# A normalised FNet + gated-MLP block: the first tile's load, its roundings and the order of the first products

## The chip, the cores and the metric

One core of a Trainium2 chip runs the kernel. The core has five engines with instruction queues of their own: TensorE (PE; its weight loads are shown as PEld), VectorE (DVE), ScalarE (ACT), GpSimd (POOL) and SyncE (SP). DMA transfers are issued from the queues of SyncE, ScalarE and GpSimd. The metric is the device time of one execution in microseconds (us). Rows of the profile count from the start of the profiled span.

## The reference, cut to what matters

```python
xn = (x - mean(x)) / sqrt(var(x) + 1e-5)            # x: 2048 x 640, over the last axis
a  = xn @ dft_hid_re.T ;  b = xn @ dft_hid_im.T     # 640 x 640
y  = dft_seq_re @ a - dft_seq_im @ b                # 2048 x 2048
gate = xn @ W_gate ;  up = xn @ W_up                # 640 x 1728
out = x + y + ((gate * (gate > 0)) * up) @ W_down   # 1728 x 640
```

All arrays are float32.

## The kernel before, in words

The products with the sequence DFT matrix come first: for each group of 256 tokens (two tiles j = 0, 1 of 128 tokens each) the normalised x is the stationary operand, 128 x 128, and a piece of 512 columns of the DFT matrix (a chunk, c) is the moving one. To keep float32 accuracy each operand is split into a high part, rounded to TensorE's 32-bit format, and a low part, what the rounding left out; a product is made of three: high x times high DFT, low x times high DFT, high x times low DFT. In the code these are v = 0, 1 and 2.

The work is listed as steps (load, prepare, run, finish), which `drive` emits in a fixed order; instructions passed through `pin` keep the order in which they are written on their engine.

The head is the part before TensorE has work. TensorE runs 44 small products (L119) to warm up. `first_stream.load` issues the first DMAs: tile 0 of x in two halves by columns, one from SyncE's queue and one from ScalarE's (L613), then tile 0's piece of chunk 0 on SyncE's queue and of chunk 1 on ScalarE's (`lead_dft`, L610), then tile 1 and its pieces on SyncE's queue. Ahead of them VectorE sets the last column of tile 0's place to zero (L611); the DMA that covers that column waits for it. `first_group` then prepares:

- VectorE: statistics of each half (`ln_stats`, L211) and their aggregate (L212);
- ScalarE: one over the root of the variance (`ln_first`, L217);
- the high part of chunk 0, tile 0: columns 0 to 255 on ScalarE, 256 to 511 on VectorE (L346, L347; ScalarE's shows under `copy`, L128);
- `raw_high(0)`, VectorE (L337): high part of the normalised x, 384 columns;
- `center(0)`, ScalarE: minus the mean (`ln_mean`, L220) and x minus mean over all 640 columns (L342);
- `high(1, 0)`, ScalarE (L332): high part of chunk 1; `low(0, 0, ...)`, VectorE (L333): low part of chunk 0;
- `ln_refine`, VectorE (L226): three one-column steps of scalar_tensor_tensor that make the root more accurate; `ln_low`, VectorE (L240): low part of the normalised x, which needs `center` and `ln_refine`;
- `low(1, 0, ...)`, GpSimd (L333): low part of chunk 1. It is put behind a VectorE memset of one element of its own output (L354), so that it starts when VectorE has come that far.

Then the same for tile 1. `first_products(j, b)` (L576) issues tile j's products in a written order of (v, chunks); each entry has three products (x blocks 0, 1 and 4) into three banks. The entries are 18 products for tile 0 and 18 for tile 1. `next_products` (L546) follows with the next group.

GpSimd also makes low parts of later groups (L281), beside which VectorE runs `ln_center` (L230) on 640 columns in some groups.

Of the kernel before, what the change touches and what calls it, by code (L numbers as in the profile page):

```python
# [7 lines left out]
F32 = mybir.dt.float32  # L8
# [4 lines left out]
P = 128  # L13
S, D, F = 2048, 640, 1728
# [49 lines left out]
def fnet_reglu_kernel(  # L64
# [56 lines left out]
    def bank():  # L121
        return psum_p.tile([P, CH], F32, name="ps")
# [4 lines left out]
    def copy(o, i):  # L127
        return nc.scalar.activation(o, i, AF.Copy)  # L128
# [64 lines left out]
    def ln_place(g):  # L193
# [2 lines left out]
        b = g % NH * SG * D  # L196
        return late["ln_tile"][:, b : b + SG * D].rearrange("p (j d) -> p j d", j=SG)

    def ln_tiles(g):
        return (ln_place(g),  # L200
                small.tile([P, SG, 2, nc.vector.BN_STATS_DIM], F32, name="bs"),
                small.tile([P, SG, 7], F32, name="mv"))

    def ln_load(g, js):
# [2 lines left out]

    def ln_stats(g, xs, bs, mv, js):
        for j in range(SG)[js]:
            for i in range(2):  # L210
                yield nc.vector.bn_stats(bs[:, j, i], xs[:, j, i * D // 2 : (i + 1) * D // 2])  # L211
            yield nc.vector.bn_aggr(mv[:, j, 0:2], bs[:, j])  # L212

    def ln_first(g, mv, js):

# [6 lines left out]
    def ln_refine(g, mv, js):  # L222

        v, r0, t = (mv[:, js, i] for i in (1, 4, 5))
        for o, i, by, op in ((t, v, EPS, OP.add), (t, t, -0.5, OP.mult), (stat[:, 1, g, js], t, 1.5, OP.add)):
            yield nc.vector.scalar_tensor_tensor(o, i, by, r0, op0=op, op1=OP.mult)  # L226
# [20 lines left out]
    def pin(steps):  # L247
        return [tc.keep_in_program_order(i) for i in steps]
# [78 lines left out]
    def first_group(b):  # L327


        xs, bs, mv = ln_tiles(0)  # L330
        part = lambda c, j: b[c][1][:, j * CH : (j + 1) * CH]
        high = lambda c, j: pin([nc.scalar.activation(b[c][0][:, 0, j], part(c, j), AF.Copy)])  # L332
        low = lambda c, j, engine: pin([engine.tensor_tensor(b[c][0][:, 1, j], part(c, j), b[c][0][:, 0, j].bitcast(F32),  # L333
                                                             op=OP.subtract)])
        j0, j1 = slice(0, 1), slice(1, 2)
        def raw_high(j):
            pin([nc.vector.tensor_scalar(ln_parts(0, j, K14)[0], xs[:, j, K14], mv[:, j, 0:1], mv[:, j, 4:5],  # L337
                                         op0=OP.subtract, op1=OP.mult)])

        def center(j):  # L340
            pin([ln_mean(0, mv, slice(j, j + 1))])
            pin([nc.scalar.activation(xs[:, j], xs[:, j], AF.Identity, bias=stat[:, 0, 0, j : j + 1])])  # L342

        pin(ln_stats(0, xs, bs, mv, j0))
        pin([ln_first(0, mv, j0)])
        for cs, rounded in ((slice(0, HC), copy), (slice(HC, CH), nc.vector.tensor_copy)):  # L346
            pin([rounded(b[0][0][:, 0, 0, cs], part(0, 0)[:, cs])])  # L347
        raw_high(0)
        center(0)
        high(1, 0)  # L350
        low(0, 0, nc.vector)
        pin(ln_refine(0, mv, j0))
        pin([ln_low(0, xs, 0, K14)])
        pin([nc.vector.memset(b[1][0][:, 1, 0, :1].bitcast(F32), 0.0)])  # L354
        low(1, 0, nc.gpsimd)
        pin(ln_stats(0, xs, bs, mv, j1))
        high(0, 1)
        pin([ln_first(0, mv, j1)])
        raw_high(1)
        high(1, 1)  # L360
        center(1)
        pin(ln_refine(0, mv, j1))
        low(0, 1, nc.vector)
        pin([ln_low(0, xs, 1, K14)])
        pin([nc.vector.memset(b[1][0][:, 1, 1, :1].bitcast(F32), 0.0)])
        low(1, 1, nc.gpsimd)
# [200 lines left out]
    def first_products(j, b):  # L567

        keys = [("e1", 0), ("e1", 1), "v1"]
        for v, cs in (((0, (0,)), (2, (0,)), (0, (1,)), (1, (0, 1)), (2, (1,))),  # L570
                      ((0, (0, 1)), (1, (0, 1)), (2, (0, 1))))[j]:
            for c in cs:
                for d, key in zip((0, 1, 4), keys):
                    if j == 0 and v == 0:
                        E[c, key] = bank()
                    pin([nc.tensor.matmul(E[c, key], xn_part(j, d)[v == 1], b[c][0][:, int(v == 2), j],  # L576
                                          start=j == 0 and v == 0, stop=False)])

    def resident(g, d):
        return lambda j, i: xn_part(g * SG + j, d + i)  # L580
# [18 lines left out]
    def first_stream(c, name, g):  # L599

        t = {}
        half = int(name == "B21")
        n = half * NH + g

        norm = {0: 0 if n == 0 else None, 1: n + 1 if n < NG - 1 else None}.get(c)

        def load():
            if n == 0 and c == 0:
                st = start["raw"] = [raw(), raw()]
                get = lambda c, j, queue=nc.sync: pin([queue.dma_start(st[c][:, j * CH : (j + 1) * CH], lead_dft[c, j, :, :CH])])  # L610
                pin([nc.vector.memset(ln_place(0)[:, 0, D - 1 :], 0.0)])  # L611
                for queue, cs in ((nc.sync, slice(0, D // 2)), (nc.scalar, slice(D // 2, D))):
                    pin([queue.dma_start(ln_place(0)[:, 0, cs], x[: SG * P].rearrange("(p j) d -> p j d", j=SG)[:, 0, cs])])  # L613
                get(0, 0)
                get(1, 0, nc.scalar)
                pin([nc.scalar.activation(root_t, eps_t, AF.Abs_reciprocal_sqrt)])
                ln_load(0, slice(1, 2))
                get(0, 1)
                get(1, 1)
                return  # L620
            if norm is not None:
                tc.keep_in_program_order(ln_load(norm, slice(0, SG)))
            if n > 0 or c > 1:
                t["s"] = raw()
                nc.sync.dma_start(t["s"], dft[c, 0, n])
                start[c, n] = t

        def prepare():
            if norm == 0:
                start["b"] = [(parts(), st) for st in start["raw"]]  # L630
                first_group(start["b"])
                return
            if (n > 0 or c > 1) and "b" not in t:
                t["b"] = b = parts()
                with ExitStack() as order:
                    if c == 1:
                        order.enter_context(tc.issue_after(late["ln"]))
                        order.enter_context(tc.issue_after(late["high"]))
                    i = split(flat(b, 0), flat(b, 1), t["s"])
                if c == 1 and n < NG - 1:  # L640
                    late["ln"] = i.ins
                    scale_a21()
            if norm is not None:
                t1 = start[0, norm]
                t1["b"] = parts()
                next_group(norm, t1["b"], t1["s"], flat(b, 1)[:, W2 - 1 : W2] if norm > 1 else None)

        def run():
            if n == 0 and c < 2:
                first_products(c, start["b"])  # L650
                return
            if n > 0 and c == 0:
                next_products(n, t["b"])
                if n == NH - 1:
                    keep_first()
                return
            accs = [(c, ("e1", i)) for i in range(2)]
            with ExitStack() as order:
                if n > 0 and c == 1:
                    order.enter_context(tc.issue_after(start["pe"]))  # L660
                product(g, t["b"], resident(n, 0), accs, half == 0, half == 1, ((c, "v1"), half, half == 0))

        def keep_first():
            t["first"] = sums_a()
            for i, key in enumerate((("e1", 0), ("e1", 1), "v1")):
                pin([copy(t["first"][:, i], E[c, key])])
            late["finish"]()

        def finish():
            if g == NH - 1:  # L670
                s = t.get("first")
                if s is None:
                    s = (sums_a, sums_b)[c % 2]()
                    for i, key in enumerate((("e1", 0), ("e1", 1), "v1")):
                        copy(s[:, i], E[c, key])
                defer(1, lambda: nc.gpsimd.dma_start(pqd[c][0][:, :3] if half else firsts[c], s[:, :3]))

        todo.append((load, prepare, run, finish))
# [225 lines left out]
    class Weights:  # L904
# [36 lines left out]
        def low(self, src, at, n, o):  # L941
            main = lambda t: t.rearrange("p (k n) -> p k n", k=n)[:, :, : 2 * P]
            tt(self.w[:, o : o + n * 2 * P].rearrange("p (k n) -> p k n", k=n), main(src), main(self.w[:, at : at + n * P3]).bitcast(F32),  # L943
               op=OP.subtract)
# [574 lines left out]
```

## Time and profile before

| | |
|---|---|
| median of 3 runs | 1019.25 us (1019.0 to 1019.42) |
| profiled execution | 1019.12 us |
| its span (first to last instruction) | 1017.3 us |
| TensorE busy | 1012.6 us |
| VectorE, ScalarE, GpSimd busy | 809.2, 488.4, 135.3 us |
| granted TensorE clock, mean | 1.00 |

The span is the profiled execution's time less what lies around the instructions. Busy times of different engines overlap. A row of a timeline has start, duration, engine, line, operation, output and input by the program's names, shapes, and in brackets the engine's idle time ahead of it with what ended that.

### The profile page before, as it was taken

The page shows a single profiled execution, that of the slowest core. Times are in us where ns is not written, and L with a number is a line of the kernel's source. Part 1 is how long each engine was busy: PE and PEld are TensorE (multiplying, and loading weights), DVE is VectorE, ACT ScalarE, POOL GpSimd, SP SyncE. Part 2 cuts the span into 40 slices and gives each one's busy share as a digit, 9 for nine tenths or more (in the row PEclk, how much of TensorE's full clock was granted, in tenths as well). Part 3 has the DMA queues.
Part 4 walks back from the last instruction along what each step waited for, and adds up shares of the span by engine and source line. Part 5 has one row for each costly group of instructions (what it writes and reads, how often), then busy time and mean ns, then how long its engine had stood idle before and what let it go on. Part 6 is the DMA issues. An engine that isn't in the chain of part 4 may idle for free.

```text
span 1017.3 us, 12622 instructions
## 1 busy us (share of the span) xinstructions
PE 1012.6 (100%) x4498; PEld 838.8 (82%) x4498; DVE 809.2 (80%) x1085; ACT 488.4 (48%) x659; POOL 135.3 (13%) x215
## 2 busy tenths in 40 slices
PE   9999999999999999999999999999999999999998
PEld 8888888888888888888888888888888888888887
DVE  7957977998989677787777988886687896767983
ACT  5654453343443334555556655565444434444432
POOL 3521001012121001222221011001000000000000
PEclk9999999999999999999999999999999999999999
DMA  8997735968979898666569877784898467896724
GB/s 321 319 293 278 267 120 172 336 217 273 349 237 353 338 358 269 232 236 220 205 214 390 291 273 284 278 308 151 318 387 288 132 243 245 285 331 203 244 79 138
DMA packets 94142, 266.43 MB, mean 262 GB/s; under 512 B 11776, under 2 KB 32832, under 8 KB 91264
## 3 DMA queue, kind: packets, MB, share of 16 engines
q1 hardware_dynamic: 73584, 185.12, 52.8%
q0 software_dynamic: 20064, 79.97, 21.5%
q8 instruction: 35, 0.57, 0.2%
q10 hardware_dynamic: 432, 0.56, 0.2%
q14 instruction: 27, 0.22, 0.1%
HBM read 198.74 MB, written 65.81 MB: 260 GB/s over the span
## 4 chain that ended last, share of the span: by engine, by line
PE 99%; DMA 0%; DVE 0%; SPq 0%; ACT 0%; issue 0%
PE ps L137 29%; PE ps L139 29%; PE ps L138 29%; PE ps L973 4%; PE ps L546 3%; PE ps L976 2%; PE ps L576 1%; PE ps L1364 1%; PE ps L1369 0%; DMA raw<-in_lead 0%; PE ps L1379 0%; DVE xs_early L337 0%; SPq L613 0%; ACT y L128 0%; DVE cb L347 0%
## 5 line engine op out<-in xcount | busy, mean ns | idle before, releaser
L131 ACT ACTIVATE cb<-rw 128x1024 fp32r<-128x1024 f32 x83 | 81.8, 988 | 138.0 <-PE ps L139 92.5
L132 DVE TENSOR_TENSOR cb<-rw,cb 128x1024 fp32r<-128x1024 f32 x83 | 93.8, 1131 | 48.2 <-ACT cb L131 47.7
L131 ACT ACTIVATE cb<-raw 128x1024 fp32r<-128x1024 f32 x71 | 75.3, 1060 | 114.5 <-PE ps L139 106.3
L132 DVE TENSOR_TENSOR cb<-raw,cb 128x1024 fp32r<-128x1024 f32 x71 | 86.8, 1223 | 39.4 <-ACT cb L131 39.2
L137 PE MATMUL ps<-cb,wt 128*128 128x512 f32 x270 | 105.0, 389 | 0.0
L138 PE MATMUL ps<-cb,wt 128*128 128x512 f32 x270 | 105.0, 389 | 0.0
L139 PE MATMUL ps<-cb,wt 128*128 128x512 f32 x270 | 105.0, 389 | 0.0
L137 PE MATMUL ps<-cb,xs_late 128*128 128x512 f32 x232 | 90.2, 389 | 0.0
L138 PE MATMUL ps<-cb,xs_late 128*128 128x512 f32 x232 | 90.2, 389 | 0.0
L139 PE MATMUL ps<-cb,xs_late 128*128 128x512 f32 x232 | 90.2, 389 | 0.0
L137 PE MATMUL ps<-cb,xs_early 128*128 128x512 f32 x226 | 87.9, 389 | 0.0
L138 PE MATMUL ps<-cb,xs_early 128*128 128x512 f32 x226 | 87.9, 389 | 0.0
L139 PE MATMUL ps<-cb,xs_early 128*128 128x512 f32 x226 | 87.9, 389 | 0.0
L128 ACT ACTIVATE gw<-z 64x512 fp32r<-64x512 f32 (+1 forms) x52 | 46.8, 899 | 49.1 <-PE ps L973 41.7
L943 DVE TENSOR_TENSOR gw<-zs,gw 128x1024 fp32r<-128x1024 f32 x26 | 31.8, 1225 | 42.7 <-ACT gw L128 42.6
L137 PE MATMUL ps<-xs_early,gw 128*128 128x512 f32 x156 | 60.7, 389 | 0.0
L138 PE MATMUL ps<-xs_early,gw 128*128 128x512 f32 x156 | 60.7, 389 | 0.0
L139 PE MATMUL ps<-xs_early,gw 128*128 128x512 f32 x156 | 60.7, 389 | 0.0
L138 PEld LDWEIGHTS ps<-cb,wt 128*128 128x128 f32 x270 | 50.7, 188 | 10.6
L128 ACT ACTIVATE ps<-ps 128x512 f32<-128x512 f32 (+1 forms) x53 | 30.6, 578 | 59.8 <-PE ps L973 55.4
L139 PEld LDWEIGHTS ps<-cb,wt 128*128 128x128 f32 x270 | 50.7, 188 | 10.5
L137 PEld LDWEIGHTS ps<-cb,wt 128*128 128x128 f32 x270 | 50.7, 188 | 10.5
(219 smaller groups left out, 2415.4 us busy)
## 6 DMA issues: line engine op xcount, KB each, us to landing
raw<-in_dft SPq DMA_DIRECT2D x94, 512.0 KB, 5.7
z<-in_wgu SPq DMA_DIRECT2D x26, 896.0 KB, 5.8
wd<-wparts SPq DMA_DIRECT2D x30, 512.0 KB, 5.1
wparts<-pw POOLq DMA_DIRECT2D x12, 1152.0 KB, 4.7
hd<-ob POOLq DMA_DIRECT2D x26, 512.0 KB, 3.9
rw<-hd SPq DMA_DIRECT2D x24, 512.0 KB, 7.4
tk<-in_dft SPq DMA_DIRECT2D x16, 512.0 KB, 8.5
set<-r POOLq DMA_DIRECT2D x16, 512.0 KB, 4.1
```

The lines of the kernel that those rows point to most:

```text
L128: return nc.scalar.activation(o, i, AF.Copy)
L131: nc.scalar.activation(hi, src, AF.Copy)
L132: return nc.vector.tensor_tensor(lo, src, hi.bitcast(F32), op=OP.subtract)
L137: nc.tensor.matmul(ps, wh, mh, start=first, stop=False, skip_group_check=more)
L138: nc.tensor.matmul(ps, wh, ml, start=False, stop=False, skip_group_check=more)
L139: nc.tensor.matmul(ps, wl, mh, start=False, stop=last, skip_group_check=more)
L546: start["pe"] = pin([nc.tensor.matmul(E[0, key], xn_part(n * SG + j, d)[v == 1], b[:, int(v == 2), j], start=False, stop=n % NH == NH - 1 ...
L576: pin([nc.tensor.matmul(E[c, key], xn_part(j, d)[v == 1], b[c][0][:, int(v == 2), j], start=j == 0 and v == 0, stop=False)])
L943: tt(self.w[:, o : o + n * 2 * P].rearrange("p (k n) -> p k n", k=n), main(src), main(self.w[:, at : at + n * P3]).bitcast(F32), op=OP.sub ...
L973: nc.tensor.matmul(ps, w[:, a * P3 + 2 * P : (a + 1) * P3], crossing[q, x], start=False, stop=last, skip_group_check=not first)
L976: nc.tensor.matmul(ps, weights[n].w5[:, a : a + P], set_half(q, X4, c)[0], start=False, stop=True, skip_group_check=True)
L1364: nc.tensor.matmul(B[out], w[:, 0, v, oo : oo + P], b[:, 0, 0], start=False, stop=last and v == 1, skip_group_check=more)
```

## The change

Tile 0 of x is loaded in three parts by columns, 0 to 215 on SyncE's queue and 216 to 431 and 432 to 639 on ScalarE's, and each part has statistics of its own; the other tiles keep two halves. Both halves of the first rounding run on ScalarE, behind one another. `high(1, 0)` goes ahead of `center(0)`; the memset and GpSimd's `low(1, 0)` go ahead of `ln_refine` and `ln_low`. Tile 0's products run in the order v = 0, 2, 1, each for both chunks, and the first three products (v = 0, chunk 0) are cut into six of 256 columns.

```diff
+    FIRST_PARTS = ((0, 216), (216, 432), (432, D))
+
+    def stat_parts(g, j):
+        return FIRST_PARTS if (g, j) == (0, 0) else ((0, D // 2), (D // 2, D))
+
     def ln_tiles(g):
         return (ln_place(g),
-                small.tile([P, SG, 2, nc.vector.BN_STATS_DIM], F32, name="bs"),
+                small.tile([P, SG, 3, nc.vector.BN_STATS_DIM], F32, name="bs"),
                 small.tile([P, SG, 7], F32, name="mv"))
@@ ln_stats
         for j in range(SG)[js]:
-            for i in range(2):
-                yield nc.vector.bn_stats(bs[:, j, i], xs[:, j, i * D // 2 : (i + 1) * D // 2])
-            yield nc.vector.bn_aggr(mv[:, j, 0:2], bs[:, j])
+            cuts = stat_parts(g, j)
+            for i, (a, b) in enumerate(cuts):
+                yield nc.vector.bn_stats(bs[:, j, i], xs[:, j, a:b])
+            yield nc.vector.bn_aggr(mv[:, j, 0:2], bs[:, j, : len(cuts)])
@@ first_group
         pin(ln_stats(0, xs, bs, mv, j0))
         pin([ln_first(0, mv, j0)])
-        for cs, rounded in ((slice(0, HC), copy), (slice(HC, CH), nc.vector.tensor_copy)):
-            pin([rounded(b[0][0][:, 0, 0, cs], part(0, 0)[:, cs])])
+        for cs in (slice(0, HC), slice(HC, CH)):
+            pin([copy(b[0][0][:, 0, 0, cs], part(0, 0)[:, cs])])
         raw_high(0)
+        high(1, 0)
         center(0)
-        high(1, 0)
         low(0, 0, nc.vector)
+        pin([nc.vector.memset(b[1][0][:, 1, 0, :1].bitcast(F32), 0.0)])
+        low(1, 0, nc.gpsimd)
         pin(ln_refine(0, mv, j0))
         pin([ln_low(0, xs, 0, K14)])
-        pin([nc.vector.memset(b[1][0][:, 1, 0, :1].bitcast(F32), 0.0)])
-        low(1, 0, nc.gpsimd)
         pin(ln_stats(0, xs, bs, mv, j1))
@@ first_products
-        for v, cs in (((0, (0,)), (2, (0,)), (0, (1,)), (1, (0, 1)), (2, (1,))),
+        for v, cs in (((0, (0, 1)), (2, (0, 1)), (1, (0, 1))),
                       ((0, (0, 1)), (1, (0, 1)), (2, (0, 1))))[j]:
             for c in cs:
-                for d, key in zip((0, 1, 4), keys):
-                    if j == 0 and v == 0:
-                        E[c, key] = bank()
-                    pin([nc.tensor.matmul(E[c, key], xn_part(j, d)[v == 1], b[c][0][:, int(v == 2), j],
-                                          start=j == 0 and v == 0, stop=False)])
+                begin = j == 0 and v == 0
+                if begin:
+                    E.update({(c, key): bank() for key in keys})
+                for at in (slice(0, HC), slice(HC, CH)) if begin and c == 0 else (slice(0, CH),):
+                    for d, key in zip((0, 1, 4), keys):
+                        pin([nc.tensor.matmul(E[c, key][:, at], xn_part(j, d)[v == 1], b[c][0][:, int(v == 2), j, at],
+                                              start=begin and at.start == 0, stop=False)])
@@ first_stream.load
-                for queue, cs in ((nc.sync, slice(0, D // 2)), (nc.scalar, slice(D // 2, D))):
+                for queue, cs in zip((nc.sync, nc.scalar, nc.scalar), (slice(*c) for c in FIRST_PARTS)):
                     pin([queue.dma_start(ln_place(0)[:, 0, cs], x[: SG * P].rearrange("(p j) d -> p j d", j=SG)[:, 0, cs])])
```

## Rows read from the trace of the kernel before

**Rows 1.** Busy times of the page: busy us, share of the span, instructions.

```profile
PE 1012.6 (100%) x4498; PEld 838.8 (82%) x4498; DVE 809.2 (80%) x1085; ACT 488.4 (48%) x659; POOL 135.3 (13%) x215
```

**Rows 2.** Stretches: length, busy time of each engine (instructions), granted clock, DMA share, GB/s.

```profile
14.00:1010.00 996.00, 996.00 (x4395) 824.39 (x4394) 798.72 (x1052) 479.14 (x640) 132.51 (x209) 1.00 0.75 262
```

**Rows 3.** Timeline of TensorE, first products and the turn to v = 1.

```profile
5.56 0.70 PE L576 MATMUL ps<-cb,xs_early 128*128 128x512 f32 x2 [0.49 <-DVE xs_early L337]
...
10.90 0.62 PE L576 MATMUL ps<-cb,xs_early 128*128 128x512 f32 x2
```

**Rows 4.** Timeline of VectorE in the head.

```profile
3.41 0.92 DVE L211 BATCH_NORM_STATS2 bs<-r 128x6 f32<-128x320 f32 x2 [2.50 <-DMA r<-in_x]
4.36 0.21 DVE L212 BATCH_NORM_AGGREGATE mv<-bs 128x2 f32<-128x12 f32 x1
4.69 0.29 DVE L347 CAST cb<-raw 128x256 fp32r<-128x256 f32 x1
4.94 0.48 DVE L337 TENSOR_SCALAR xs_early<-r,mv 128x384 fp32r<-128x384 f32 x1
5.33 0.69 DVE L333 TENSOR_TENSOR cb<-raw,cb 128x512 fp32r<-128x512 f32 x1
5.93 0.35 DVE L226 SCALAR_TENSOR_TENSOR mv<-mv 128x1 f32<-128x1 f32 x2
...
6.59 0.62 DVE L240 SCALAR_TENSOR_TENSOR xs_early<-r,stat,xs_early 128x384 fp32r<-128x384 f32 x1
...
7.16 0.06 DVE L354 MEMSET cb<- 128x1 f32 x1
7.55 0.47 DVE L211 BATCH_NORM_STATS2 bs<-r 128x6 f32<-128x320 f32 x1
...
8.63 0.48 DVE L337 TENSOR_SCALAR xs_early<-r,mv 128x384 fp32r<-128x384 f32 x1 [0.36 <-ACT mv L217]
...
10.11 0.62 DVE L240 SCALAR_TENSOR_TENSOR xs_early<-r,stat,xs_early 128x384 fp32r<-128x384 f32 x1
```

**Rows 5.** Timeline of ScalarE in the head.

```profile
4.61 0.30 ACT L217 ACTIVATE mv<-mv,eps_t 128x1 f32<-128x1 f32 x1 [1.27 <-DVE mv L212]
4.81 0.40 ACT L128 ACTIVATE cb<-raw 128x256 fp32r<-128x256 f32 x1
5.11 0.19 ACT L220 ACTIVATE stat<-mv 128x1 f32<-128x1 f32 x1
5.50 0.83 ACT L342 ACTIVATE r<-r,stat 128x640 f32<-128x640 f32 x1 [0.20 <-ACT stat L220]
6.24 0.61 ACT L332 ACTIVATE cb<-raw 128x512 fp32r<-128x512 f32 x1
```

**Rows 6.** Timeline of the first issues on ScalarE's queue (ACTq).

```profile
0.85 0.06 DVE L611 MEMSET r<- 128x1 f32 x1
0.95 0.38 ACTq L613 DMA_DIRECT2D r<-in_x  x1
...
1.36 0.45 ACTq L610 DMA_DIRECT2D raw<-in_lead  x1
```

**Rows 7.** DMA issues from 0.7 to 1.5: size each, us to landing.

```profile
raw<-in_lead ACTq DMA_DIRECT2D x1, 256.0 KB, 3.9
...
r<-in_x ACTq DMA_DIRECT2D x1, 160.0 KB, 2.8
```

**Rows 8.** Chain that ended last, half-width products at its end: start, us, what.

```profile
1012.94 0.24 PE ps L1379 x2
```

**Rows 9.** Timeline of GpSimd in the head.

```profile
7.38 1.28 POOL L333 TENSOR_TENSOR cb<-raw,cb 128x512 fp32r<-128x512 f32 x1 [6.92 <-DVE cb L354]
```

**Rows 10.** L230: durations ns min/median/max from 40 us; then timelines from 41.6 to 43.7.

```profile
L230 DVE TENSOR_SCALAR r<-r,mv x6: 501/1420/1585, 41.7 to 57.6; 128x640 f32<-128x640 f32 x6
...
41.71 2.00 DVE L230 TENSOR_SCALAR r<-r,mv 128x640 f32<-128x640 f32 x2
...
41.77 1.59 POOL L281 TENSOR_TENSOR cb<-raw,cb 128x512 fp32r<-128x512 f32 x1
```

## The prediction

> **What bounds the kernel now.** I read the page's busy table first: TensorE is busy for all but 4.7 us of the span [rows 1]. The table of stretches then shows that after the head it has no idle time, at a granted clock of 1.00, the 2.4 GHz level [rows 2]. So the kernel ends as late as the first products begin, plus TensorE's work, plus whatever stalls are put between: a delay in the head is never made up, and a gain there is kept in full. The change touches nothing else, so the rest is read from the timelines of the first 14 us, engine by engine.
>
> TensorE ends its warming products, waits 0.49 us for raw_high (L337) and starts at 5.56 [rows 3]. Behind raw_high stand, on VectorE, two statistics (3.41, together 0.92) and their aggregate (4.36 to 4.57) [rows 4], then ScalarE's root (4.61 to 4.91) [rows 5]. VectorE rounds half of the first chunk from 4.69 to 4.98 and starts raw_high at 4.94 [rows 4]: that rounding stands in front of it, but the root has come only 0.03 before. I write R for the end of raw_high, 5.42 before. TensorE starts at R+0.14.
>
> **The load in three parts.** Before, ScalarE's first DMA issue (0.95) waits for VectorE's one-column memset of L611 (0.85), since its half holds that column [rows 6]; after, the column is in the third part, so the second part may be issued at about 0.75 and the third, 0.41 behind (the distance of the two issues), between 1.16 and 1.36. ScalarE's lead load goes one issue later. ScalarE idles 1.27 us ahead of its root [rows 5], which covers the longer issuing.
>
> When the third part lands is the open number. The nearest rows: on this queue 160 KB landed 2.8 us after its issue, at 3.75, and the 256 KB behind it 3.9 us after, at 5.26 [rows 6, 7]. That is 1.51 us for 256 KB, so 212 KB (parts two and three) would be in at 3.75 + 52 x 1.51/256 = 4.06, or 0.2 sooner if the issue is: 3.9. Bounds: 3.75 (as the half landed) and 5.26 (as the second transfer of that queue landed). Its statistic takes about 0.4, so at 3.9 it ends at 4.3, and VectorE's own work decides: two statistics took 0.92, 0.46 each; the aggregate of 12 columns takes 0.21 [rows 4], so some 0.15 of each instruction does not depend on columns, and a third instruction adds 0.15: 3.41 + 1.07 = 4.48 against 4.33 before. The first part is 108 KB in place of 160 and lands a little earlier; I take **+0.1** on R, with bounds of -0.1 (no cost for the third instruction, first part 0.1 earlier) and +1.3 (third part at 5.26, 0.4 for its statistic: 5.66 against 4.33). R is then 5.52.
>
> **Roundings on ScalarE.** Taking the rounding off VectorE gains at most 0.03 (above): nothing. On ScalarE the two halves follow the root: a half took 0.40, the next instruction started 0.30 behind it, and the first half started 0.20 behind the root's start [rows 5]. R is 0.81 behind the root's start [rows 4, 5], so the second half ends at 0.20 + 0.30 + 0.40 = 0.90, R+0.09. Three short products come first, so it is in time. The chunk itself, which the rounding had at 4.69 at the latest [rows 4], is needed no earlier than before, and 52 KB less lie ahead of it in SyncE's queue.
>
> **Six short products.** The trace has half-width ones at its end: two take 0.24 [rows 8], so six take 0.72 against three times 0.23 [rows 3]: **+0.04**.
>
> **The other order.** VectorE's low of chunk 0 needs the second half: R+0.13 to R+0.82 (0.69), 0.22 later than before (5.33) [rows 4]. High of chunk 1 now goes ahead of mean and centre: R to R+0.61 (before 6.24 [rows 5]); TensorE wants it at R+0.14+0.72. Its load is issued one place later behind 52 KB more, so at 5.26 + 0.3 = R+0.04: covered. Centre moves behind it: mean at R+0.52, centre R+0.75 to R+1.58, 0.67 later than before (5.50 to 6.33) [rows 5].
>
> GpSimd's low of chunk 1 follows VectorE's memset by 0.22 and takes 1.28 [rows 4, 9]. The memset stood behind ln_low (7.16, R+1.74); now it stands behind low of chunk 0, R+0.77. GpSimd runs R+0.99 to R+2.27. TensorE, which by its rate in the early products comes to those low products at R+2.33, gets them at about R+2.4: a stall of **0.1**, and the low products of x (v = 1) are due at R+3.1.
>
> What decides is that VectorE's three refine steps and ln_low, which read two operands each from SBUF, now stand beside GpSimd's operation, which reads two as well. Before, GpSimd's operation had only statistics and their aggregate beside it (it ended at 8.67, raw_high began at 8.63), and they kept their 0.47 [rows 4, 9]. No row shows a two-operand VectorE operation beside it. The nearest one is L230: 128x640 takes 0.50 at the least and 1.58 at the most, and of the two from 41.71 to 43.71 the second ends 0.35 behind GpSimd's operation (43.36) [rows 10]. It waits to that operation's end and then runs. From both sides:
>
> - *No hold.* ln_low starts behind centre: R+1.62 to R+2.24, hidden (due R+3.1). The second tile's raw_high ends 1.90 behind ln_low (7.21, 9.11 [rows 4]): R+4.14, due R+4.46 less 0.14: hidden. Its ln_low ends 1.62 later (10.73 [rows 4]): R+5.76, TensorE R+5.90.
> - *Hold.* The refine steps start at R+0.74, 0.19 apart (5.93 [rows 4]), so the third meets GpSimd's operation and waits. GpSimd ends at R+2.27 to 2.37; the third step, then ln_low (0.12 and 0.62 [rows 4]), ends at R+3.14; if only ln_low is held, at R+2.74 (0.35 of its run plus a little behind GpSimd's end). I take R+3.0. TensorE goes on at R+3.14. The statistics of tile 1 stand behind ln_low: raw_high at R+4.90, TensorE at R+5.04, free since R+4.50: a stall of 0.54. Centre and ln_low of tile 1: R+6.52, TensorE R+6.66, free since R+6.40: another 0.26.
>
> Before, TensorE began these last low products at 11.13 [rows 3], R+5.71. So no hold costs 5.90 - 5.71 = 0.19, and hold 6.66 - 5.71 = **0.95** (0.69 to 1.09). The short products and the stalls lie inside these. I take hold, as in the nearest row.
>
> By the Trainium skill (SBUF — State Buffer, section "SBUF: two separate sides") the port pair that VectorE and GpSimd share is an exclusive lock for a whole instruction, and a VectorE operation with two SBUF inputs takes it against a GpSimd operation that reads SBUF. L230's 1.58 against 0.50 agrees for one kind of operation; for two inputs no run shows it. With that rule the sum is the hold's, without it the other.
>
> Behind the head, VectorE is some 1.1 to 1.2 us later and TensorE 1.05, so the next group's waits are as loose as they were within 0.15. The eight-deep reuse of the load semaphores moves by one place, which delays SyncE's next issues by a few tenths while the loads are limited by bytes: nothing.
>
> **Sum.** 0.1 + 0.95 = 1.05 us on the profiled execution's 1019.12 (span 1017.3, 1.8 around it): **1020.2**. The median of the three runs is 1019.25, 0.13 above that execution; the runs spread over 0.4. Changes under 0.2%, 2.04 us, can hardly be told from none.
>
> **Rivals.**
> - *No hold* (21%): 0.1 + 0.19 = 0.3, so 1019.4. For it: the statistics run beside GpSimd undisturbed. Against it: they read one operand; L230 is held.
> - *The third part lands late* (6%, the slower side): as the second transfer of its queue it lands at 5.26, R is 1.3 later, and with hold the sum is 1019.12 + 1.3 + 0.95 = 1021.4. It decides from a landing at about 5.2 on (R 1.2 later passes 1021.29). For it: the second transfer of that queue did land then. Against it: that one was 256 KB, this is 104.
> - *The parts do what they seem made for and nothing is held* (6%): R 0.1 earlier with no hold, 1019.1 to 1019.3. A gain above 0.2% (1%) is shut out: TensorE's whole wait ahead of its first product is 0.49 us.
>
> **How the numbers follow.** The forecast, hold and a third part in time, has 66%, its own range 1019.8 to 1020.9. With no hold at the lower end and half of the late landing at the upper, the range is 1019.3 to 1021.1, which leaves out some 13%. Faster 0.01, same 0.93, slower 0.06: only the late landing passes the bound.
>
> **What would show it.** In the profile after: three statistics from about 3.35, the last ending near 4.45; TensorE starting near 5.66, not before 5.4; GpSimd's first operation near 6.5, and beside it a refine step or ln_low that lasts past 1 us; TensorE idle about 0.5 us ahead of tile 1's products and 0.2 to 0.3 ahead of its low ones; the first product of L546 near 14.9 in place of 13.85. An ln_low of 0.62 beside a running GpSimd means no hold, and L546 near 14.15. If the last statistic waits for the third part past 4.5, the size of R's shift is wrong. A total outside the range with a head that moved under 1.5 us would mean that something behind the head changed, and I have named nothing there.

## The result and the profile after

| | before | after |
|---|---|---|
| median of 6 runs, us | 1019.12 (1018.91 to 1019.62) | 1023.41 (1021.75 to 1024.76) |
| ratio, 95% interval | | 1.0041 [1.0030, 1.0052] |
| profiled execution, its span, us | 1019.12, 1017.3 | 1024.06, 1022.3 |
| granted clock, mean | 1.00 | 0.998 |

The changed kernel is 0.41% slower; the range said 1019.3 to 1021.1. Its six runs spread over 3 us, and each trace below is of one execution. One run of a later kernel (e11), 1272.91 us at a granted clock of 0.753, is left out of that kernel's median. The timeline of TensorE after (the lines answer to [rows 3]) has the loss in three places:

```profile
6.15 0.95 PE L584 MATMUL ps<-cb,xs_early 128*128 128x256 f32 x6 [1.28 <-ACT cb L128]
9.67 9.41 PE L584 MATMUL ps<-cb,xs_early 128*128 128x512 f32 x33 [2.57 <-ACT cb L338]
18.91 1.29 PE L552 MATMUL ps<-cb,xs_early 128*128 128x512 f32 x5
...
10.72 2.77 PE L584 MATMUL ps<-cb,xs_early 128*128 128x512 f32 x6
```

The six short products start at 6.15 (5.56 before). Then TensorE waits 2.57 us for the high part of chunk 1 (`high(1, 0)`, now L338). The next group's first product (L552 after, L546 before) starts at 18.91, before at 13.85. The last line is a stretch behind the wait: six products, of which the last takes 0.63, so their starts are (2.77 - 0.63)/5 = 0.43 apart, where they were 0.23 apart before. The table of stretches (length, busy time of each engine, granted clock, DMA share, GB/s) shows the clock there:

```profile
8.00:10.00 2.00, 0.33 (x1) 0.30 (x2) 0.00 (x0) 0.98 (x3) 0.30 (x1) 1.00 1.01 407
10.00:12.00 2.00, 2.00 (x7) 1.57 (x6) 1.39 (x3) 1.09 (x2) 0.99 (x1) 0.66 1.03 428
12.00:14.00 2.00, 2.00 (x6) 1.62 (x5) 1.53 (x7) 1.48 (x4) 0.00 (x0) 0.50 1.02 419
14.00:16.00 2.00, 2.00 (x10) 1.58 (x10) 1.97 (x7) 1.21 (x3) 0.93 (x1) 0.98 1.03 426
```

TensorE was busy 0.95 us of the 4.8 between the last warming product and 9.67; about 1 us behind its restart the granted clock falls to 0.50, the 1.2 GHz level, and it is back at 14.1. Why it waited stands in ScalarE's timeline (answers to [rows 5]) and in the landings of the first issues (answers to [rows 7]):

```profile
5.20 0.29 ACT L223 ACTIVATE mv<-mv,eps_t 128x1 f32<-128x1 f32 x1 [1.55 <-DVE mv L218]
5.40 0.71 ACT L128 ACTIVATE cb<-raw 128x256 fp32r<-128x256 f32 x2
8.99 0.63 ACT L338 ACTIVATE cb<-raw 128x512 fp32r<-128x512 f32 x1 [2.88 <-DMA raw<-in_lead]
```

```profile
r<-in_x SPq DMA_DIRECT2D x1, 320.0 KB, 6.3
raw<-in_lead SPq DMA_DIRECT2D x1, 256.0 KB, 3.1
raw<-in_lead ACTq DMA_DIRECT2D x1, 256.0 KB, 7.3
r<-in_x ACTq DMA_DIRECT2D x1, 108.0 KB, 2.7
r<-in_x SPq DMA_DIRECT2D x1, 108.0 KB, 2.5
r<-in_x ACTq DMA_DIRECT2D x1, 104.0 KB, 3.2
```

Chunk 1's lead, which is tile 0's piece of chunk 1, is now third on ScalarE's queue. It took 7.3 us from its issue, 3.9 before. The chain that ended last runs through it (1.67 is its issue):

```profile
1.67 7.29 DMA raw<-in_lead
...
8.99 0.64 ACT cb L338
...
9.67 9.41 PE ps L584 x33
```

VectorE (answers to [rows 4]) waits for the third part, and later for the centre behind the late high part:

```profile
3.29 0.67 DVE L217 BATCH_NORM_STATS2 bs<-r 128x6 f32<-128x216 f32 x2 [2.38 <-DMA r<-in_x]
4.52 0.38 DVE L217 BATCH_NORM_STATS2 bs<-r 128x6 f32<-128x208 f32 x1 [0.55 <-DMA r<-in_x]
4.93 0.24 DVE L218 BATCH_NORM_AGGREGATE mv<-bs 128x2 f32<-128x18 f32 x1
5.53 0.48 DVE L343 TENSOR_SCALAR xs_early<-r,mv 128x384 fp32r<-128x384 f32 x1 [0.36 <-ACT mv L223]
...
10.61 0.80 DVE L246 SCALAR_TENSOR_TENSOR xs_early<-r,stat,xs_early 128x384 fp32r<-128x384 f32 x1 [3.31 <-ACT r L348]
```

The sum: 6.15 - 5.56 = 0.59 for the later start. From the first product to the first one behind chunk 0's high part it is 9.67 - 6.15 = 3.52, where the three full products took 0.77 before (the fourth started at 6.33): 2.75 for the wait, the short products' 0.04 in it. The 33 products behind took 18.91 - 9.67 = 9.24 where they took 13.85 - 6.33 = 7.52: 1.72, nearly all of it the low clock. 0.59 + 2.75 + 1.72 = 5.06 = 18.91 - 13.85; the profiled executions differ by 4.94.

### The profile page after: what moved, and what is told of

Its sections match the earlier page's. It is cut to its first block, busy times and chain, and to the rows that moved or that the text cites. A ratio compares the mean times of both kernels' runs of the same rounds, so it can differ in the third digit from the quotient of the medians.

```text
span 1022.3 us, 12633 instructions
## 1 busy us (share of the span) xinstructions
PE 1014.3 (99%) x4501; PEld 840.1 (82%) x4501; DVE 810.2 (79%) x1085; ACT 488.7 (48%) x660; POOL 134.8 (13%) x215
## 4 chain that ended last, share of the span: by engine, by line
PE 99%; DMA 1%; ACT 0%; ACTq 0%; issue 0%
PE ps L139 29%; PE ps L138 29%; PE ps L137 29%; PE ps L981 4%; PE ps L552 3%; PE ps L984 2%; PE ps L584 1%; DMA raw<-in_lead 1%; PE ps L1372 1%; PE ps L1377 0%; ACTq L621 0%; ACT cb L338 0%; PE ps L1387 0%; ACT y L128 0%
```

## The experiments

Two theories after the result. **L**: the load's new place in the queues makes chunk 1's lead late, and the wait and the clock follow from it. **O**: the new order of the work costs it. All runs in one table; "lead" is where chunk 1's lead landed, "next group" where its first product started, "GB/s" the mean traffic from 3.5 to 8.5 us, all of the one profiled execution; the median and the ratio are over the runs of each kernel against runs of before on the same chip.

| kernel | median us | ratio [95%] | lead | next group | GB/s |
|---|---|---|---|---|---|
| before | 1019.12 | | 5.2 | 13.85 | 383 |
| changed | 1023.41 | 1.0041 [1.0030, 1.0052] | 9.0 | 18.91 | 284 |
| e1 two halves again | 1020.05 | 1.0010 [1.0001, 1.0020] | 5.0 | 14.74 | 378 |
| e2 three parts alone | 1021.23 | 1.0019 [1.0009, 1.0028] | 8.0 | 16.73 | 332 |
| e3 third part on SyncE | 1021.14 | 1.0019 [1.0009, 1.0028] | 4.6 | 15.36 | 403 |
| e4 issue waits as before | 1022.84 | 1.0036 [1.0023, 1.0049] | 8.2 | 17.84 | 312 |
| e5 two uneven parts | 1020.36 | 1.0014 [1.0004, 1.0023] | 6.6 | 15.42 | 356 |
| e6 before, tiny third | 1020.48 | 1.0013 [1.0003, 1.0022] | 8.5 | 16.17 | 375 |
| e7 before, lead second of three | 1019.28 | 1.0001 [0.9992, 1.0010] | 5.0 | 14.33 | 398 |
| e8 48 filler products | 1023.88 | 1.0044 [1.0029, 1.0059] | 7.6 | 17.49 | 335 |
| e9 tile 1's x last | 1023.77 | 1.0043 [1.0028, 1.0058] | 8.2 | 18.75 | 307 |
| e10 all on SyncE | 1020.83 | 1.0016 [1.0006, 1.0025] | 5.8 | 15.50 | 291 |
| e11 two halves, GpSimd back | 1019.41 | 1.0003 [0.9993, 1.0012] | 5.5 | 14.20 | 363 |
| e12 16 filler products | 1021.95 | 1.0028 [1.0017, 1.0039] | 7.9 | 16.77 | 329 |
| e13 cuts at 256 and 512 | 1022.54 | 1.0032 [1.0019, 1.0045] | 7.1 | 15.95 | 319 |
| e14 lead ahead of third part | 1024.69 | 1.0052 [1.0037, 1.0067] | 5.1 | 19.50 | 383 |
| e15 three parts alone, third on SyncE | 1021.10 | 1.0016 [1.0006, 1.0026] | 5.1 | 16.44 | 385 |
| e16 before again | 1019.05 | 0.9998 [0.9988, 1.0007] | 5.0 | 14.15 | 373 |

The time of each profiled execution less its "next group" is 1005.1 to 1005.3 us in all eighteen: nothing behind the head differs in any of them.

**e1: load undone, the rest as changed.**

```diff
-    FIRST_PARTS = ((0, 216), (216, 432), (432, D))
+    FIRST_PARTS = ((0, D // 2), (D // 2, D))
-                for queue, cs in zip((nc.sync, nc.scalar, nc.scalar), ...
+                for queue, cs in zip((nc.sync, nc.scalar), ...
```

> The changed kernel with tile 0 loaded in two halves again (two statistics), all else as changed. Theory L (the three-part load makes chunk 1's lead land late, and all of the loss follows from that landing): the lead lands near 5.2 us as before, first product near 5.6, no idle of 2.6 us, granted clock 1.00 throughout, and the time is 1019.1 plus what the new order costs by itself, 0.2 to 1.0 us: 1019.3 to 1020.1. Theory O (the new order costs it, the lead is late by chance or whatever the load): the time stays within 1 us of the changed kernel's 1023.4.

1020.05: theory L, as far as the changed kernel goes. Without the load the whole of the wait is gone. (Seven of e1's runs lie at 1019.9 to 1020.1, the profiled one among them, and three at 1021.3, of which no trace was kept.) What is left, 0.8 us, is the new order's own, and VectorE's timeline has it where the prediction put it, beside GpSimd's operation (second fence, GpSimd's timeline):

```profile
6.04 0.15 DVE L232 SCALAR_TENSOR_TENSOR mv<-mv 128x1 f32<-128x1 f32 x1
...
6.23 0.16 DVE L232 SCALAR_TENSOR_TENSOR mv<-mv 128x1 f32<-128x1 f32 x1
6.42 1.17 DVE L232 SCALAR_TENSOR_TENSOR stat<-mv 128x1 f32<-128x1 f32 x1
7.71 0.62 DVE L246 SCALAR_TENSOR_TENSOR xs_early<-r,stat,xs_early 128x384 fp32r<-128x384 f32 x1
```

```profile
6.28 1.29 POOL L339 TENSOR_TENSOR cb<-raw,cb 128x512 fp32r<-128x512 f32 x1 [5.82 <-DVE mv L232]
```

The third one-column step takes 1.17 in place of 0.16 and ends at 7.59, 0.02 behind GpSimd's operation (7.57).

**e2: the three-part load alone, in the kernel before.** The edit is the load's and the statistics' part of the change.

> The kernel before with the three-part load and its statistics alone. Theory L: the lead lands at 7 us or later and TensorE waits for chunk 1, now behind six full-width products, so the loss is nearly the whole of it, 3 to 5 us: 1022 to 1024. Theory O: the third part costs what its landing costs the root, 0.6 us: 1019.7, lead in by 5.6.

The lead landed at 8.0, as theory L said, but the time, 1021.23, is 0.8 under its range, and the lead costs nothing here: its high part was ready at 8.7, and the first product that needs it starts at 9.6. TensorE's one wait, 1.27 us, is for raw_high. The chain of e2 runs through the third part of x, in at 5.18, so the first product starts at 6.92, 1.36 later than before:

```profile
1.21 3.97 DMA r<-in_x
...
6.92 9.98 PE ps L582 x36
```

The rest is TensorE's pace. The 36 products of tiles 0 and 1 take 16.73 - 6.92 = 9.81 where they took 13.85 - 5.56 = 8.29 before, 1.52 more, and 1.36 + 1.52 = 2.88 = 16.73 - 13.85. Stretches of 3 us of e2 and, below it, of before (columns as above):

```profile
7.00:10.00 3.00, 3.00 (x7) 2.36 (x8) 2.41 (x10) 2.18 (x5) 1.23 (x1) 1.00 1.03 404
6.00:9.00 3.00, 3.00 (x15) 2.38 (x14) 2.41 (x10) 2.18 (x5) 1.28 (x1) 1.00 1.02 406
```

Both rows give a clock of 1.00, yet 7 products stand against 15: e2's start 0.43 apart, the pace of the 1.2 GHz level. At the start of a trace the 1.00 is no reading. The warming products too start 0.11 apart at first and 0.06 apart later, all at 1.00, because the trace has no record of the clock before its first one. That record stands where the pace rises: at 4.24 before, at 3.5 to 6.4 in fifteen other kernels, and only at 10.2 in e2 and 10.0 in e15.

**e3, e4: which side of the load.** e3 issues the third part on SyncE's queue, so that the lead is second on ScalarE's; e4 gives ScalarE's first issue its wait back.

```diff
e3: zip((nc.sync, nc.scalar, nc.scalar), ...  ->  zip((nc.sync, nc.scalar, nc.sync), ...
e4: nc.vector.memset(ln_place(0)[:, 0, D - 1 :], 0.0)  ->  nc.vector.memset(ln_place(0)[:, 0, 431:432], 0.0)
```

> The changed kernel with the third part issued on SyncE's queue (behind the first part, ahead of chunk 0's lead), so that chunk 1's lead is again second on ScalarE's queue. Theory L in the form 'third place on ScalarE's queue': the lead lands by 5.5 us and the time is 1019.5 to 1020.5. Theory L in the form 'three parts that are issued at the same moment disturb the transfers': still late, 1022 or more.

> The changed kernel with VectorE's one-column memset on a column of the second part, so that ScalarE's first DMA issue waits for it again (0.95 in place of 0.75 us). If the earlier, simultaneous issue of both queues is what disturbs the transfers: lead by 5.7 us and 1020 to 1020.5. If it is the third transfer on that queue: lead at 7 us or later and 1022 to 1024.5.

e3's lead was in at 4.6, its profiled execution took 1020.52; the median, 1021.14, is 0.6 over the range given and 2.3 under the changed kernel's. e4 keeps its loss with its lead at 8.2: the moment of the first issue is not the cause, the lead's place is.

**e5, e6, e7: transfers or bytes on ScalarE's queue.**

```diff
e5, on the changed kernel, with (nc.sync, nc.scalar) as queues:
-    FIRST_PARTS = ((0, 216), (216, 432), (432, D))
+    FIRST_PARTS = ((0, 216), (216, D))
e6, on the kernel before:
-  ((nc.sync, slice(0, D // 2)), (nc.scalar, slice(D // 2, D)))
+  ((nc.sync, slice(0, D // 2)), (nc.scalar, slice(D // 2, D - 16)), (nc.scalar, slice(D - 16, D)))
e7, on the kernel before:
                 get(1, 0, nc.scalar)
+                get(0, 1, nc.scalar)
...
-                get(0, 1)
```

> The changed kernel with tile 0 in two uneven parts: columns 0 to 215 on SyncE's queue, 216 to 639 on ScalarE's, so ScalarE's queue carries the changed kernel's bytes in two transfers in place of three. Theory N (a third transfer on ScalarE's queue is what makes the loads lag): chunk 1's lead lands by 5.6 us and the time is 1020 to 1021. Theory Y (the bytes ahead of the lead on that queue): lead at 7.5 us or later, 1022 to 1024.

> The kernel before with ScalarE's half of tile 0 cut into two transfers, 304 and 16 columns; statistics, products and order as before. Theory N: the lag is there although no byte moved to another queue: chunk 1's lead at 7 us or later, 1020 to 1022. Theory Y: lead by 5.6 us; the small third transfer delays the root by 0.4 us at most, 1019.2 to 1019.7.

> The kernel before with tile 1's piece of chunk 0 issued third on ScalarE's queue, behind chunk 1's lead, in place of SyncE's queue: three transfers on ScalarE's queue, the lead still second. Theory N: transfers that are under way with the third lag by 1 to 3 us (tile 1's pieces land at 8.5 us or later in place of 7.1 and 7.7), while chunk 1's lead lands near 5.2 us; 1019.5 to 1021.5. Theory Y: nothing lags, 1019.2.

Neither theory has it alone. More bytes ahead in two transfers bring the lead in at 6.6, 1.3 later than before; a transfer of 8 KB ahead of it, with no byte moved to another queue, makes it 8.5. In e7 the lead, second, is in at 5.0 and the time is that of before, while the third transfer lands at 8.4. Over all runs: the third transfer on ScalarE's queue landed between 6.9 and 9.0 us in the ten kernels that have one, whatever it was, and the lead as second between 4.6 and 6.6 in the nine that have it there.

The place on ScalarE's queue is not the only thing that these kernels change. Before, the lead was issued at 1.36 [rows 6] and SyncE's 320 KB of tile 1 behind it; in the changed kernel, and likewise in e6, they go out together. SyncE's issue before, then both issues after:

```profile
1.67 0.43 SPq L206 DMA_DIRECT2D r<-in_x  x1
...
1.66 0.42 SPq L211 DMA_DIRECT2D r<-in_x  x1
1.67 0.45 ACTq L618 DMA_DIRECT2D raw<-in_lead  x1
```

Counted over both queues, 576 KB or less were issued ahead of the lead in ten kernels, and it was in at 4.6 to 6.6. In the other eight 832 or 896 KB were issued ahead of it or within 0.01 us of it, and it was in at 7.1 to 9.0. In all eighteen traces the transfers issued up to 2.7 us land in the order of their issue over both queues, but for pairs issued within 0.02 us of each other. This is read from single executions, and it does not give the size: before, tile 1's x had 832 KB ahead of it and was in at 6.0.

**e8, e12: the clock.** Small products into a bank of their own behind the six short ones:

```diff
+                if begin and c == 0:
+                    filler = bank()
+                    for _ in range(FILL):        # e8: 48, e12: 16
+                        pin([nc.tensor.matmul(filler[:, :P], warm, warm, start=True, stop=True)])
```

> The changed kernel with 48 of the small warming products put behind the six short ones, into a bank of their own, so that TensorE is not idle while chunk 1's lead is late. If the lower granted clock behind the wait (0.66 and 0.50 from 10 to 14 us) is caused by that idle time and costs 1.7 us: clock 1.00 throughout and 1021 to 1022.2. If the clock falls for another reason or costs nothing: 1023 to 1024.5.

> The changed kernel with 16 small warming products (about 1.0 us) behind the six short ones, in place of 48 that outlasted the wait. If it is the idle time that takes the clock down: granted clock 1.00 through 14 us and products 0.23 us apart behind the wait; the time is then 0.5 to 1.7 us under the changed kernel's, 1021.7 to 1023. If not: products 0.43 us apart for some 3 us, 1023 to 1024.8.

e8's fillers ran to about 10 while the lead's high part was ready at 8.3, so they cost about what the clock would have: its time says nothing, its clock was 1.00. e12's ended with the wait, 8.6; its stretches (columns as above):

```profile
8.00:10.00 2.00, 2.00 (x19) 1.64 (x17) 0.46 (x1) 1.97 (x4) 1.29 (x1) 1.00 1.00 410
10.00:12.00 2.00, 2.00 (x11) 1.60 (x9) 1.60 (x5) 0.62 (x3) 0.00 (x0) 1.00 1.04 429
12.00:14.00 2.00, 2.00 (x9) 1.15 (x7) 1.93 (x8) 1.97 (x4) 0.00 (x0) 1.00 1.03 421
```

Clock 1.00 throughout and products at the full pace, 1021.95: 1.5 under the changed kernel's median. None of the 11 runs of e8 and e12 has a mean granted clock under 0.999; four of the changed kernel's six runs and all nine of e4 and e9 have 0.998 or less. So idle TensorE is what takes the clock down. Its price is the 1.72 us of the changed kernel's trace; the 1.5 between the medians also holds the lead's landing, 7.9 in e12's trace against 9.0.

**e9, e10: what makes the loads lag.** In the changed kernel not the lead alone is late: SyncE's transfers of tile 1 land at 8.0 to 9.8 (6.0 to 7.7 before), and the traffic from 3.5 to 8.5 us is down:

```profile
DMA packets 720, 1.42 MB, mean 284 GB/s; under 512 B 89, under 2 KB 153, under 8 KB 720
```

e9 issues tile 1's x behind the leads of tile 1; e10 puts the first five transfers all on SyncE's queue.

```diff
e9:
-                ln_load(0, slice(1, 2))
                 get(0, 1)
                 get(1, 1)
+                ln_load(0, slice(1, 2))
e10:
-  zip((nc.sync, nc.scalar, nc.scalar), ...
+  zip((nc.sync, nc.sync, nc.sync), ...
...
-                get(1, 0, nc.scalar)
+                get(1, 0)
```

> The changed kernel with tile 1's x load issued behind tile 1's two leads on SyncE's queue, so that other data than tile 1's x runs beside chunk 1's lead. If the lag comes of tile 1's x beside the other transfers: chunk 1's lead by 6 us, 1020 to 1021.3. If it comes of two queues working at once, whatever they carry: lead at 7.5 us or later, mean traffic from 3.5 to 8.5 us under 340 GB/s, 1022 to 1024.5.

> The changed kernel with all three parts and both leads on SyncE's queue, nothing on ScalarE's. If two queues at once make the lag: no lag, mean traffic from 3.5 to 8.5 us 390 GB/s or more, chunk 1's lead by 6 us in spite of its later issue, 1020 to 1021.3. If three small parts make it, whatever the queue: lead at 7.5 us or later, 1022 or more.

e9: it is not tile 1's x alone, for with SyncE's first lead of tile 1 issued in its place (1.67) the lag is the same. e9's time comes another way, though: the third part was in at 5.55, TensorE waited 2.57 us ahead of its first product (7.29), the granted clock was down from 6.9 to 13.7, and there is hardly a wait for chunk 1's lead. e10: it is not two queues at once, for the traffic was 291 GB/s on one; yet the lead, fifth on SyncE's queue and issued only at 2.61 but ahead of tile 1's x (3.08), was in at 5.8 and the time is 1020.83. In the new order the place decides the time, the lag has another cause.

**e11: GpSimd's operation back behind ln_low, in e1, and chunk 1's products with low DFT last.**

```diff
         pin(ln_refine(0, mv, j0))
         pin([ln_low(0, xs, 0, K14)])
+        pin([nc.vector.memset(b[1][0][:, 1, 0, :1].bitcast(F32), 0.0)])
+        low(1, 0, nc.gpsimd)
-        for v, cs in (((0, (0, 1)), (2, (0, 1)), (1, (0, 1))),
+        for v, cs in (((0, (0, 1)), (2, (0,)), (1, (0, 1)), (2, (1,))),
```

> The two-halves version of the changed kernel (1020.0, 0.8 above before) with the memset and GpSimd's operation behind ln_low again, and chunk 1's products with low DFT behind those with low x. Hold theory: VectorE's third refine step takes 0.16 in place of 1.17 us, the 0.8 is gone: 1018.9 to 1019.4, first product of the next group at 13.7 to 13.9 us. Rival (the roundings in halves, high ahead of centre and the short products cost it): 1019.8 to 1020.2.

1019.41 against 1019.08: not to be told from before. The third step takes 0.16 again. The next group started at 14.20, 0.54 earlier than in e1 and 0.3 later than I expected: VectorE now waits 0.45 for the centre, which stands behind high(1, 0). Most of e1's 0.8 was the hold.

**e13 to e16: the lag again.** e13 cuts at 256 and 512 columns; e14 issues the lead ahead of the third part on ScalarE's queue; e15 is e2 with the third part on SyncE's queue; e16 is the kernel before.

```diff
e13:
-    FIRST_PARTS = ((0, 216), (216, 432), (432, D))
+    FIRST_PARTS = ((0, 256), (256, 512), (512, D))
e14, inside the loop over the parts, in place of the two calls behind it:
+                    if n_part == 2:
+                        get(0, 0)
+                        get(1, 0, nc.scalar)
```

> The changed kernel with the parts cut at columns 256 and 512 (1024, 1024 and 512 bytes a row). If the odd sizes make the lag: traffic from 3.5 to 8.5 us 375 GB/s or more, chunk 1's lead by 6 us, 1020 to 1021.3. If not: traffic under 340 GB/s, lead at 7 us or later, 1022 to 1024.5.

> The changed kernel with chunk 1's lead issued ahead of the third part on ScalarE's queue. If the lead's place decides the time: lead by 5.5 us, the wait of 2.6 us and the low clock are gone; the third part lands later instead, near 5.3 us, so the first product starts near 7 and the time is 1021 to 1022. If the lag follows the three parts and hits what is needed next: third part at 6.5 us or later, 1022 to 1024.

> The kernel before with the three-part load, its third part on SyncE's queue. If the third part's place on ScalarE's queue makes the lag: traffic 375 GB/s or more, chunk 1's lead by 5 us, and the time is that of a root 0.5 us later, 1019.4 to 1020.1. If any three-part load lags: 1020.5 to 1022.

> The kernel before, unchanged, beside the other three. If the lag happens by chance in any execution: traffic from 3.5 to 8.5 us may be under 340 GB/s here too, with little effect on the time since its leads are in before it starts. If it belongs to the three parts: 375 GB/s or more. Time 1019.0 to 1019.5 either way.

e13: the odd sizes are not the cause (319 GB/s, lead at 7.1). e14: the lead is in at 5.1, but now the third part, third on the queue, lands at 6.9, the first product starts at 8.65 and the time is the worst of all: what is third on that queue, here issued 0.02 behind tile 1's x, is late, and the time follows what needs it; the clock was at 0.50 from 7.4 to 14.2. e15: traffic 385, lead at 5.1; its median, 1021.10, missed my 1019.4 to 1020.1 and is no better than e2's 1021.23 with the lead at 8.0: with the three-part load in the old order the lead's place is worth nothing that these runs show. (In e6, also the old order, TensorE does wait 1.12 us for chunk 1.) e15's runs fall in two groups, four from 1019.43 to 1019.67 and six from 1020.67 to 1022.39; the trace is of the second, with the first product at 6.54 (0.98 later than before) and 9.90 us for the 36 products, 1.61 more, at the low pace until 10.0. What the first group did no trace shows. e16: 373 GB/s, 1019.05.

## Why the prediction was wrong

**The step that failed** is in the other order's part: "Its load is issued one place later behind 52 KB more, so at 5.26 + 0.3 = R+0.04: covered." The lead landed at 8.96, R+2.95. I had counted the bytes ahead in ScalarE's own queue and taken the rate from its first two transfers. One place later, the lead is issued together with SyncE's 320 KB of tile 1, which before went out behind it; over both queues 896 KB are ahead of it in place of 576, and none of the ten third transfers was in before 6.9. That moving the lead back ends the wait is shown in the new order by e1, e3 and e10 (1020.05 to 1021.14). The new order put products that need this lead directly behind the six short ones, and high(1, 0) ahead of the centre, so the wait stood in front of everything: 2.6 us. By the Trainium skill (DMA: Bandwidth & Descriptors, section "Issuing engines are not separate DMA queues") transfers of all issuing engines interleave on the same 16 DMA engines; e5 to e7 agree in that a queue's own bytes do not tell when a transfer lands.

**What was missing** is the clock. I took the granted clock as 1.00 and had no rival in which it falls; 1.72 of the 5.06 us between the two traces are products at the 1.2 GHz level, and e12 shows what took the clock down. Nor had I one in which the clock rises late, the 1.5 and 1.6 us of e2's and e15's traces. Before, TensorE had 0.49 us of idle time in the head; with 1.3 us ahead of the short products and 2.6 behind them it fell.

**Mis-sized**: the third part's landing, 3.9 taken (bounds 3.75 and 5.26), came at 4.4; R moved by 0.6 in place of 0.1. The step is the same: this part is issued 0.02 behind SyncE's 256 KB of chunk 0 and landed 0.17 behind them, and I had left them out. In e2, e4, e8, e9, e12 and e13 it came at 4.5 to 5.6, past the upper bound in e9. The third statistic added less than the 0.15 taken: two take 0.67 and one 0.38, so three take 0.96 against 0.92. The late-landing rival had the right kind of mechanism, a late transfer on ScalarE's queue, on the wrong transfer.

**Right**: the last rounding ends at 6.11, R+0.10 (said: R+0.09); the short products are 0.12 apart; the cast cost nothing to lose. The hold exists, and its size shows in e1, where the load does not cover it: sum 0.95, measured 14.74 - 13.85 = 0.89 and 0.8 in the medians, and 1.17 for the third step. (e1's R is 5.29; counted from R it is 1.02, and ln_low ends at R+3.04 where I said R+3.0.) That step reads two one-column operands, so the lock that the Trainium skill states for two SBUF inputs (SBUF — State Buffer, "SBUF: two separate sides") is shown by e1. In the changed kernel itself the hold cost little: GpSimd started at 9.70, and ln_low (0.80 in place of 0.62) was held for some 0.2 of its run.

**Open**: why traffic falls to 284 to 335 GB/s between 3.5 and 8.5 us in the changed kernel, e2, e4, e8 to e10, e12 and e13, and stays at 356 to 403 in the other ten. In the first eight chunk 1's lead is issued behind two or three parts of x on its queue; e6, where it is too, has 375. That is a correlation over single profiles. The count of transfers, the bytes, tile 1's x, two queues and odd sizes were each tried and none is the cause alone. So the order of issue says which transfers wait, and why the lead then lands 3.7 us later in the changed kernel stays open. Open too is what made the clock rise late in e2 and e15.

## What to carry to other kernels

A transfer's landing is not read from the bytes ahead of it in its own queue: put first on a queue what the first consumer needs, and add up what all queues together have issued ahead of it. Where a reorder puts a consumer directly behind a short piece of work, look up the landing of everything it reads, with the latest seen in the trace as the bound. Idle time on TensorE in a head costs twice when the granted clock falls behind it, so such a rival belongs in the list whenever an edit can leave TensorE waiting. Where a row gives a clock of 1.00 at a kernel's start, check it by the distance of the products' starts.

## What the runs showed of the hardware that I had not expected

- TensorE's granted clock fell to 0.50 after 1.28 us idle, 0.95 busy and 2.57 idle (changed kernel); in e4 after 1.25, 0.95 and 1.29; in e12, with 1.29 idle and then no wait to speak of, it stayed at 1.00.
- A one-column VectorE step with two SBUF operands, begun 0.14 us behind a GpSimd operation, ends 0.02 behind it (1.17 against 0.16 us).
- A transfer of 8 KB ahead of the lead on ScalarE's queue went with a landing at 8.5 us in place of 5.2 (e6), at 375 GB/s of traffic over the stretch, hardly less than before; it had moved the lead's issue from 1.36 to 1.67, 0.01 behind tile 1's x.
